# Rebuilding fp32 weights from 64-bit words: the last addition moved from GpSimd to VectorE, the sign mask made a 16-bit operation, one attention scaling moved to GpSimd

## The chip, the cores and the metric

One core of one Trainium2 chip runs the whole program. The metric is device time in microseconds (us); the median of several runs is compared. Engines are named as the profile names them: PE (TensorE matmul), PEld (its weight load), DVE (VectorE), ACT (ScalarE), POOL (GpSimd), SP (the engine that issues most DMAs). L705 is line 705 of the kernel before.

## The reference

Attention over 4 batches, 8 heads, 576 positions and 64 columns, mixed with a linear-attention memory, and then two feed-forward layers over 2304 tokens:

```python
a = softmax(causal(q @ k.T / sqrt(D)))
local = a @ v
mem_out = (phi(q) @ M_prev) / (phi(q) . z_prev)       # phi = elu + 1
x = g * mem_out + (1 - g) * local                     # 2304 x 512
h1 = x @ w_in1;  y = (s * relu(h1)**2 + b) @ w_out1   # 512 -> 2048 -> 512
h2 = y @ w_in2;  out = (h2 * tanh(softplus(h2))) @ w_out2
```

The four weight matrices of the feed-forward layers reach the core as 64-bit floats (two 32-bit words an element). Everything else is fp32.

## The kernel before, in words

The kernel splits each fp32 operand of the large products into a rounded part and a remainder ("hi" and "lo"), and TensorE makes three products in place of one.

**Stages.** The attention is cut into 32 units, one for each batch and head. Those of batch 0 are cut again into halves: eight first halves (query tiles 0 to 2, `TA`) and eight second halves (tiles 3 and 4, `TB`). These 16 are called early; their scores are plain fp32 products. The other 24 units (batches 1 to 3) run after them, in turn with the small blocks of layer 1, until about 475 us. Then come the large blocks of layer 1, and from about 620 us layer 2, whose products are written as 7 in place of 8 by combined sub-matrices.

**Conversion.** `convert` rebuilds fp32 from 64-bit words, in pieces of 128 by 512. It runs 32 times for layer 1 (to about 178 us, beside the early units) and 32 times for layer 2 (about 490 to 625 us). One piece: a DMA brings the words into a `raw` buffer; ACT scales the high word as a float (L695) into a buffer `w` of the ring `w32`, which has two slots; ACT turns the low word into a rounded integer in place (L700); DVE shifts `w` left by 3 (L702); DVE takes the sign bit of the high word and joins it to `w` (L703); POOL adds the rounded low word to `w` as an integer (L705). For layer 1, ACT then rounds `w` into the hi part (L712) and DVE subtracts for the lo part (L715); for layer 2, DVE makes sums of sub-matrices (L741), which are stored, some after a split into hi and lo (L726, L727).

**Early units.** POOL takes min(q, 0) (L498), ACT the exponential, DVE the maximum and sum (L500) and a product with a row sum for each tile (L492). PE makes the scores, DVE adds the mask and finds the least value of the row (L543), POOL writes a scaled copy of the memory's part (L555), ACT takes the exponential with a row sum (L552), DVE adjusts and inverts the sums (L572, L574). Then the rows of each tile are scaled (L569), by an engine that a letter of `E_NORM` (early units) or `F_NORM` (the others) gives for each tile: P is POOL, D is DVE, A is ACT. Tile t has 64 + 128 t columns, so 64, 192 and 320 for the tiles of a first half. PE transposes the scaled tiles (L596), ACT or DVE copies them out of PSUM (L601), and PE multiplies them with the values (L624).

**Order.** Each step has an engine, an estimated time and a priority. `Plan.order` plays the steps through with these estimates and writes down the order in which they start; each engine then runs its instructions strictly in that order. An estimate changes an order, never a duration on the chip. Conversions of layer 1 have priorities 3 to 4 apart, early units 2.36 and 8.58 apart. A first product of layer 1 can start when all eight first halves and the first weights are done; between 7 and 85 us PE is given products of zeros (L1239) where it has nothing else.

Of the kernel before, what the change touches and what calls it, by code (L numbers as in the profile page):

```python
# [11 lines left out]
BF16 = mybir.dt.bfloat16  # L12
I32 = mybir.dt.int32
U32 = mybir.dt.uint32
AF = mybir.ActivationFunctionType
ALU = mybir.AluOpType
PSUM = bass.MemoryType.PSUM
# [2 lines left out]
P = 128  # L20
MASKED = -1.0e30
HUGE = 3.0e38
SIGN = -0x80000000
PE, ACT, DVE, POOL, DMA = range(5)


# [8 lines left out]
CONV = (3.0, 3.81, 4.18, 3.12)  # L35
CONV2 = 655.2

E_TRA, E_NORM, E_XS = 'AAAADA', 'PPDDA', 'A'
F_NORM = 'PPDDA'
C_HI, C_W, C2_W = 'AAAA', 'AAAA', 'AAAA'  # L40

# [8 lines left out]
def act_us(n, extra=0):  # L50
    return 0.094 + 0.00083 * n + 0.093 * extra


def dve_us(n, fast=False):
    return 0.068 + (0.00052 if fast else 0.00104) * n


def pool_us(n):
    return 0.2 + 0.0033 * n
# [6 lines left out]
def on(letter):  # L66
    return {"A": ACT, "D": DVE, "P": POOL}[letter]
# [111 lines left out]
class Plan:  # L179
# [29 lines left out]
    def add(self, engine, us, prio, f, r=(), w=(), after=(), keep=(), share=1.0):  # L209


        bufs = list({id(b): b for b in (*r, *w, *keep) if b.ring is not None}.values())
        new = [b for b in bufs if b.maker is None]
        waits = {id(s): s for b in r for s in b.writers}
        waits.update((id(s), s) for s in after)
        s = Step(engine, us, prio, f, list(waits.values()), bufs, new)
        s.share = share
        s.left = len(waits)
        for x in waits.values():
            x.next.append(s)  # L220
        for b in bufs:
            b.users += 1
            if b.maker is None:
                b.maker = s
            elif id(b.maker) not in waits:
                b.maker.next_start.append(s)
                s.left += 1
        for b in w:
            b.writers.append(s)
        self.steps.append(s)  # L230
        return s
# [100 lines left out]
def attention_then_two_ffn(ctx: ExitStack, tc: tile.TileContext, qk, qz, vm, beta,  # L332
# [3 lines left out]
    nc = tc.nc  # L336
# [24 lines left out]
    add = plan.add  # L361
# [31 lines left out]
    nc.vector.tensor_scalar_min(igate[:, 1], igate[:, 1], 80.0)  # L393
    nc.scalar.activation(igate, igate, AF.Exp)
    nc.vector.tensor_scalar_add(igate, igate, 1.0)
# [36 lines left out]
    def unit(b, h, prio, groups=(TA, TB), place=None):  # L432
# [4 lines left out]
        def add(engine, us, f, r=(), w=(), keep=(), share=1.0):  # L437
            attention_steps.append(plan.add(engine, us, prio, f, r, w, keep=keep, share=share))
# [48 lines left out]
        def q_rows():  # L487
            return qn()[:, lo_t + 1:lo_t + n_t + 1]
# [9 lines left out]
        add(POOL, pool_us(n_t * D), lambda: nc.gpsimd.tensor_scalar_min(ex.t[:, mine], q_rows(), 0.0), [qn_b], [ex])  # L498
        add(ACT, act_us(n_t * D), lambda: nc.scalar.activation(ex.t[:, mine], ex.t[:, mine], AF.Exp), [ex], [ex])
        add(DVE, dve_us(n_t * D), lambda: nc.vector.scalar_tensor_tensor(ex.t[:, mine], q_rows(), 0.0, ex.t[:, mine],  # L500
# [26 lines left out]
        def score(t):  # L527
# [23 lines left out]
            def exp():  # L551
                nc.scalar.activation(Pt[t].t[:, D:w + D], Pt[t].t[:, D:w + D], AF.Exp, bias=mx.t[:, t + i:t + i + 1],  # L552
                                     scale=-1.0, accum_out=rs.t[:, t:t + 1])
# [5 lines left out]
        def norm(tiles):  # L559
# [4 lines left out]
            def scale(t, e):  # L564
                x, r = Pt[t].t[:, D:P * (t + 1)], rs.t[:, t:t + 1]
                if e == ACT:
                    nc.scalar.activation(x, x, AF.Copy, scale=r)
                else:
# [95 lines left out]
    def w_at(nm, r, j):  # L664
        return W[nm, r].t[:, j]
# [8 lines left out]
    def convert(layer, prio, which, r, j, raw, after=()):  # L674


        w_in, w_out = ((w_in1, w_out1), (w_in2, w_out2))[layer - 1]
        fc = r * FPR + j
        src = w_in[j * P:(j + 1) * P, r * 512:(r + 1) * 512] if which == "in" else w_out[fc * P:(fc + 1) * P, :]
        w = Buf(R["w32"], [P, 512], I32)  # L680

        def words():
            return raw.t[:, :1024].rearrange("p (n two) -> p n two", two=2)

        def f32():
            return w.t.bitcast(F32)

        add(DMA, 1.5, prio, lambda: nc.sync.dma_start(words(), src.bitcast(I32).rearrange("p (n two) -> p n two", two=2)),
            w=[raw], after=after).lag = 1.0 if layer == 1 else 3.0

        e = on((C_W if layer == 1 else C2_W)[j])
        add(e, 0.52 if e == ACT else 0.335, prio,
            (lambda: nc.scalar.activation(f32(), words()[:, :, 1].bitcast(F32), AF.Copy, scale=2.0 ** -112)) if e == ACT else  # L695
            (lambda: nc.vector.tensor_scalar(f32(), words()[:, :, 1].bitcast(F32), 2.0 ** -112, None, op0=ALU.mult)),
            [raw], [w])

        low_words = Buf()
        add(ACT, 0.52, prio, lambda: nc.scalar.activation(words()[:, :, 0], words()[:, :, 0].bitcast(U32), AF.Copy,  # L700
                                                          scale=2.0 ** -29), [raw], [low_words])
        add(DVE, 0.335, prio, lambda: nc.vector.tensor_scalar(w.t, w.t, 3, None, op0=ALU.logical_shift_left), [w], [w])  # L702
        add(DVE, 0.6, prio, lambda: nc.vector.scalar_tensor_tensor(w.t, words()[:, :, 1], SIGN, w.t,  # L703
                                                                   op0=ALU.bitwise_and, op1=ALU.bitwise_or), [raw, w], [w])
        add(POOL, 1.23 if layer == 1 else 1.45, prio, lambda: nc.gpsimd.tensor_tensor(w.t, w.t, words()[:, :, 0], op=ALU.add),  # L705
            [raw, low_words, w], [w])
        if layer == 1:
            hi, lo = f"w{which[0]}h", f"w{which[0]}l"
            hi_dve, lo_dve = C_HI[j] == "D", C_LO[j] == "D"
            half = Buf()  # L710
            add(DVE if hi_dve else ACT, 0.335 if hi_dve else 0.52, prio,
                lambda: (nc.vector.tensor_copy if hi_dve else nc.scalar.copy)(w_at(hi, r, j), f32()), [w],  # L712
                [W[hi, r], half])
            add(DVE if lo_dve else POOL, 0.6 if lo_dve else 1.23, prio,
                lambda: (nc.vector if lo_dve else nc.gpsimd).tensor_tensor(w_at(lo, r, j), f32(),  # L715
                                                                           w_at(hi, r, j).bitcast(F32), op=ALU.subtract),
                [w, half], [W[lo, r]])
        return w
# [414 lines left out]
    for i, p in enumerate(pieces):  # L1133
        convert(1, start, *p, raws[i])
        start += CONV[i // 8]
# [15 lines left out]
    for i in range(len(seq) + LAG1):  # L1151
        if i < len(seq):
# [5 lines left out]
            n = len(plan.steps)  # L1158
# [4 lines left out]
        if i >= LAG1:  # L1163
            j, fc = seq[i - LAG1]
            n = len(plan.steps)
# [3 lines left out]
            if fc == NFC - 1:  # L1169
                n = len(plan.steps)  # L1170
# [17 lines left out]
    n = len(plan.steps)  # L1188
# [3 lines left out]
    def converted_piece(which, r, j):  # L1192
        n = len(plan.steps)
        w = convert(2, CONV2, which, r, j, Buf(R["raw"], [P, 1024], I32), [opened])
        raw_steps.extend(plan.steps[n:])
        return w
# [17 lines left out]
    n = len(plan.steps)  # L1214
# [72 lines left out]
```

## Time and profile before

| | us |
|---|---|
| median of 3 runs (1041.0 to 1042.43) | 1041.44 |
| the profiled execution: its own time | 1041.25 |
| the profiled execution: span of its instructions | 1039.4 |
| busy in the span: PE | 1004.7 |
| busy in the span: DVE | 845.4 |
| busy in the span: ACT | 713.2 |
| busy in the span: POOL | 278.2 |

The span runs from the first to the last instruction of the profiled execution; 1.85 us of its own time lie around it. A busy time is the union of the engine's instructions, and an instruction that stands still because another engine keeps it from its memory still counts as busy. So a duration is read against other durations of the same instruction. PE's ends are modelled, and a busy PE is not always a PE at its peak.

### The profile page before, as it was taken

Reading aid. Unit: us, or ns where it says so; the run is one execution under the profiler, and the core shown is the slowest. Engines: PE = TensorE matmul, PEld = TensorE weight load, DVE = VectorE, ACT = ScalarE, POOL = GpSimd, SP = SyncE. Lnnn points to the kernel's source line nnn. Section 1 sums busy time; section 2 is a strip of 40 time slices with the busy share of each in tenths; the row PEclk is TensorE's granted clock in tenths of the full one; section 3 lists DMA queues with packets and bytes.
Section 4 is the critical chain, followed back from the end, with each engine's and each line's share of the span. In section 5 each row is a group of like instructions: output and inputs, shape, how many; then the busy total and the mean of one; then the engine's idle time right before and its main releaser. Section 6 shows DMA issues by size and latency. Waiting matters only on the chain.

```text
span 1039.4 us, 20180 instructions
## 1 busy us (share of the span) xinstructions
PE 1004.7 (97%) x6708; PEld 928.9 (89%) x6708; DVE 845.4 (81%) x2347; ACT 713.2 (69%) x1606; POOL 278.2 (27%) x386
## 2 busy tenths in 40 slices
PE   6889997999999999999999999999999999999998
PEld 4657787999999999999888778899999999999998
DVE  6899899999999989986568896359985789767864
ACT  6876897888988888876777897536753456434552
POOL 6864354333343334320234220000110000100010
PEclk9998998999999999999999999999999999999999
DMA  9663563323432333225888887558686766676464
GB/s 260 181 195 103 152 193 95 111 85 99 137 111 72 93 119 94 83 64 157 234 254 265 271 290 232 213 192 288 214 295 226 233 220 202 238 236 216 151 218 168
DMA packets 88984, 188.63 MB, mean 181 GB/s; under 512 B 8752, under 2 KB 63024, under 8 KB 81584
## 3 DMA queue, kind: packets, MB, share of 16 engines
q1 hardware_dynamic: 81392, 135.95, 42.3%
q0 software_dynamic: 7056, 51.38, 14.7%
q8 instruction: 53, 0.87, 0.3%
q14 instruction: 51, 0.42, 0.1%
q10 hardware_dynamic: 432, 0.01, 0.0%
HBM read 144.32 MB, written 42.99 MB: 180 GB/s over the span
## 4 chain that ended last, share of the span: by engine, by line
PE 59%; DVE 14%; issue 11%; ACT 7%; DMA 4%; POOL 3%; POOLq 0%; DVEq 0%; ACTq 0%; SPq 0%
PE bank L1003 15%; PE bank L1069 12%; PE bank L871 12%; PE bank L798 11%; PE bank L624 3%; PE bank L596 3%; DVE PTl L604 2%; PE bank L538 1%; DVE Pt L543 1%; PE bank L539 1%; DVE stage L703 1%; ACT PTh L601 1%; ACT Pt L552 1%; DVE stage L702 1%; POOL stage L705 1%
## 5 line engine op out<-in xcount | busy, mean ns | idle before, releaser
L1069 PE MATMUL bank<-woh,S 128*128 128x256 f32 x792 | 107.3, 283 | 0.0
L1069 PEld LDWEIGHTS bank<-woh,S 128*128 128x128 f32 x792 | 100.8, 192 | 0.1
L1069 PE MATMUL bank<-wol,S 128*128 128x256 f32 x720 | 98.1, 283 | 0.0
L555 POOL TENSOR_SCALAR Pt<-ex,nm 128x64 f32<-128x64 f32 x148 | 74.5, 516 | 85.1 <-PE bank L596 38.5
L1003 PE MATMUL bank<-wi,woh 128*128 128x384 f32 x426 | 94.0, 335 | 0.0
L552 ACT ACTIVATE Pt<-Pt,mx 128x64 f32<-128x64 f32 (+4 forms) x148 | 81.8, 555 | 16.5 <-DVE mx L543 15.7
L1069 PEld LDWEIGHTS bank<-wol,S 128*128 128x128 f32 x720 | 91.8, 192 | 0.0
L596 PE MATMUL bank<-ident,Pt 128*128 128x128 f32 x432 | 67.0, 281 | 10.8 <-POOL Pt L569 7.9
L1003 PEld LDWEIGHTS bank<-wi,woh 128*128 128x128 f32 x426 | 75.6, 188 | 0.6
L1003 PE MATMUL bank<-wi,wol 128*128 128x384 f32 x294 | 76.0, 335 | 0.1
L705 POOL TENSOR_TENSOR stage<-stage 128x512 int32<-128x512 int32 x36 | 48.5, 1348 | 99.6 <-DVE stage L703 50.0
L604 DVE TENSOR_TENSOR PTl<-bank,PTh 128x128 fp32r<-128x128 f32 (+1 forms) x144 | 63.8, 480 | 2.3 <-ACT PTh L601 1.2
L596 PEld LDWEIGHTS bank<-ident,Pt 128*128 128x128 f32 x432 | 49.7, 143 | 17.0 <-POOL Pt L569 10.3
L569 POOL TENSOR_SCALAR Pt<-Pt,rs 128x64 f32<-128x64 f32 x64 | 45.3, 749 | 70.7 <-DVE rs L574 54.6
L984 POOL DMA_DIRECT2D wol<-wo_split_d x17 | 9.2, 542 | 201.7 <-DVE wi L727 109.9
L543 DVE CUSTOM_DVE_ANT_0 Pt<-bank,mask 128x320 f32<-128x320 f32 (+3 forms) x148 | 59.1, 416 | 3.3 <-PE bank L539 1.6
L601 ACT CAST PTh<-bank 128x128 fp32r<-128x128 f32 (+1 forms) x144 | 54.8, 430 | 2.6 <-PE bank L596 1.7
L871 PE MATMUL bank<-gh,wol 128*128 128x256 f32 x320 | 54.0, 292 | 0.0
L871 PE MATMUL bank<-gl,woh 128*128 128x256 f32 x320 | 53.7, 290 | 0.0
L1003 PEld LDWEIGHTS bank<-wi,wol 128*128 128x128 f32 x294 | 53.0, 188 | 0.6 <-DMA wol<-wi_split_d 0.3
L871 PE MATMUL bank<-gh,woh 128*128 128x256 f32 x320 | 53.1, 289 | 0.0
L798 PE MATMUL bank<-xh,wi 128*128 128x256 f32 x320 | 50.6, 289 | 1.4 <-DVE rt L849 1.3
(278 smaller groups left out, 2961.9 us busy)
## 6 DMA issues: line engine op xcount, KB each, us to landing
wol<-wo_split_d POOLq DMA_DIRECT2D x17, 1024.0 KB, 5.2
woh<-wo_split_d POOLq DMA_DIRECT2D x16, 1024.0 KB, 5.8
qk<-in_qk SPq DMA_DIRECT2D x24, 608.0 KB, 3.9
stage<-in_w_out SPq DMA_DIRECT2D x23, 512.0 KB, 4.5
wo_split_d<-high SPq DMA_DIRECT2D x44, 256.0 KB, 3.1
stage<-in_w_in SPq DMA_DIRECT2D x21, 512.0 KB, 4.8
stage<-wi_d SPq DMA_DIRECT2D x24, 384.0 KB, 5.3
wi_split_d<-woh SPq DMA_DIRECT2D x8, 1024.0 KB, 4.9
```

The costliest lines, as they stand in the source:

```text
L543: nc.vector.tensor_tensor_reduce(Pt[t].t[:, D + lo:D + hi], ps.t[:, :hi - lo], mask[:, SP - w + lo:SP - w + hi], -SCALE, mx.t[:, t:t + 1] ...
L552: nc.scalar.activation(Pt[t].t[:, D:w + D], Pt[t].t[:, D:w + D], AF.Exp, bias=mx.t[:, t + i:t + i + 1], scale=-1.0, accum_out=rs.t[:, t:t ...
L555: add(POOL, 0.3, lambda: nc.gpsimd.tensor_scalar(Pt[t].t[:, :D], ex.t[:, t, :], nm.t[:, t:t + 1], 1.0, op0=ALU.mult, op1=ALU.mult), [ex, n ...
L569: (nc.vector if e == DVE else nc.gpsimd).tensor_scalar(x, x, r, None, op0=ALU.mult)
L596: nc.tensor.transpose(ps.t[:, c - c0, :], Pt[t].t[:, c * P:(c + 1) * P], ident)
L601: (nc.vector.tensor_copy if dve else nc.scalar.copy)(PT[0].t[:, at_], ps.t[:, :n])
L604: nc.vector.tensor_tensor(PT[1].t[:, at_], ps.t[:, :n], PT[0].t[:, at_].bitcast(F32), op=ALU.subtract)
L705: add(POOL, 1.23 if layer == 1 else 1.45, prio, lambda: nc.gpsimd.tensor_tensor(w.t, w.t, words()[:, :, 0], op=ALU.add), [raw, low_words, ...
L798: nc.tensor.matmul(ph, w_at(nm, r, cc)[:, o:o + P], x_at(x, cc), start=(part == 0 and cc == 0), stop=(part == 2 and cc == NCC - 1))
L871: nc.tensor.matmul(acc[ec // per].t[:, (ec % per) * n:(ec % per + 1) * n], w_at(nm, r, jj)[:, ec * P:(ec + 1) * P], t(x), start=(big and f ...
L1003: nc.tensor.matmul(ps.t[:, :H2], w[i // 4].t[:, j, kk, i % 4], x[kk].t[:, k], start=begin and part == kk == 0, stop=part == 2 and kk == 1, ...
L1069: nc.tensor.matmul(acc[t].t[:, :DH], s.t[:, j, t * P:(t + 1) * P], x.t[:, k, q % 4], start=q == part == 0, stop=q == NQ2 - 1 and part == 2)
```

## The change

The integer addition of a conversion goes from GpSimd to VectorE. The sign bit no longer goes into `w` by a 32-bit operation with two inputs: a 16-bit operation takes the top 16 bits of the high word, keeps bit 15, and writes it into the top 16 bits of the rounded low word, so that the addition brings the sign along. This operation waits for ACT's rounding of the low word (L700), whose result it writes into; the addition waits for it. The scaling of tile 2 of the eight first halves (320 columns) goes from VectorE to GpSimd (`E_NORM`). The estimates that the planner uses change with the steps, and with them the orders of all engines.

```diff
+U16 = mybir.dt.uint16
-SIGN = -0x80000000
-E_TRA, E_NORM, E_XS = 'AAAADA', 'PPDDA', 'A'
+E_TRA, E_NORM, E_XS = 'AAAADA', 'PPPDA', 'A'
...
+        def limbs():
+            return raw.t[:, :1024].bitcast(U16).rearrange("p (n four) -> p n four", four=4)
+
...
         add(DVE, 0.335, prio, lambda: nc.vector.tensor_scalar(w.t, w.t, 3, None, op0=ALU.logical_shift_left), [w], [w])
-        add(DVE, 0.6, prio, lambda: nc.vector.scalar_tensor_tensor(w.t, words()[:, :, 1], SIGN, w.t,
-                                                                   op0=ALU.bitwise_and, op1=ALU.bitwise_or), [raw, w], [w])
-        add(POOL, 1.23 if layer == 1 else 1.45, prio, lambda: nc.gpsimd.tensor_tensor(w.t, w.t, words()[:, :, 0], op=ALU.add),
-            [raw, low_words, w], [w])
+        signed = Buf()
+        add(DVE, 0.335, prio, lambda: nc.vector.tensor_scalar(limbs()[:, :, 1], limbs()[:, :, 3], 0x8000, None, op0=ALU.bitwise_and),
+            [raw, low_words], [signed])
+        add(DVE, 0.75, prio, lambda: nc.vector.tensor_tensor(w.t, w.t, words()[:, :, 0], op=ALU.add), [raw, signed, w], [w])
```

## Rows read from the trace of the kernel before

**Rows 1.** Busy time of each engine by stretch (busy us, count; TensorE clock, DMA)
```profile
0.00:60.00 60.00, 48.39 (x236) 33.39 (x237) 47.24 (x189) 43.99 (x125) 49.05 (x71) 1.00 0.76 216
60.00:180.00 120.00, 106.88 (x675) 88.06 (x674) 112.70 (x326) 95.52 (x220) 52.40 (x61) 0.95 0.48 146
...
250.00:300.00 50.00, 49.66 (x399) 48.17 (x398) 48.05 (x185) 42.69 (x115) 19.38 (x31) 1.00 0.38 111
```

**Rows 2.** The chain that ended last, 0:60 and 60:180, shares by line
```profile
by line: POOL stage L705 7.2%; POOL Pt L569 7.1%; DMA wil<-in_w_out 6.9%; POOL Pt L555 5.5%; issue 4.1%; POOL ex L498 3.7%; DVE stage L703 2.8%; DVE wol L492 2.5%; PE bank L534 2.5%; PE bank L596 2.3%; POOL B L555 1.8%; PE bank L1239 0.6%; 
...
by line: issue 10.6%; PE bank L798 7.2%; PE bank L871 6.1%; DVE stage L703 6.1%; PE bank L624 5.6%; DVE Pt L543 4.4%; PE bank L534 4.1%; DVE stage L702 3.7%; DVE qn L492 3.6%; DMA wil<-in_w_out 3.5%; DVE wil L715 2.9%; DVE gl L854 2.2%; DVE
```

**Rows 3.** Busy time by stretch of the additions of L705 alone
```profile
0.00:60.00 60.00, 13.28 (x10) 1.00 0.76 216
60.00:180.00 120.00, 28.93 (x22) 0.95 0.48 146
```

**Rows 4.** Timeline of VectorE and of GpSimd near 92 us (start, us, instruction)
```profile
92.21 1.76 DVE L715 TENSOR_TENSOR wil<-stage,wih 128x512 fp32r<-128x512 f32 x1
...
92.13 1.29 POOL L705 TENSOR_TENSOR stage<-stage 128x512 int32<-128x512 int32 x1 [1.61 <-ACT wih L712]
```

**Rows 5.** Instructions by line and form, VectorE, 0:180 (busy us, mean ns, idle before)
```profile
L702 DVE TENSOR_SCALAR stage<-stage 128x512 int32<-128x512 int32 x32 | 17.0, 535 | 1.6 <-ACT stage L695 1.3
L703 DVE SCALAR_TENSOR_TENSOR stage<-stage 128x512 int32<-128x512 int32 x22 | 16.2, 737 | 0.2
L715 DVE TENSOR_TENSOR wol<-stage,woh 128x512 fp32r<-128x512 f32 x16 | 12.8, 797 | 0.2 <-ACT woh L712 0.2
L492 DVE CUSTOM_DVE_ANT_0 qn<-ex,qn 128x64 f32<-128x64 f32 x31 | 8.3, 315 | 0.1
...
L715 DVE TENSOR_TENSOR wil<-stage,wih 128x512 fp32r<-128x512 f32 x8 | 7.1, 885 | 0.9 <-ACT wih L712 0.7
...
L715 DVE TENSOR_TENSOR wi<-stage,wi 128x512 fp32r<-128x512 f32 x8 | 6.4, 794 | 0.0
...
L572 DVE TENSOR_SCALAR rs<-rs,igate 128x2 f32<-128x2 f32 x10 | 5.7, 572 | 1.0 <-ACT Pt L552 0.8
...
L569 DVE TENSOR_SCALAR Pt<-Pt,rs 128x448 f32<-128x448 f32 x6 | 4.6, 763 | 0.1
```

**Rows 6.** The same view, VectorE, 180:480
```profile
L492 DVE CUSTOM_DVE_ANT_0 qn<-ex,qn 128x64 f32<-128x64 f32 x105 | 17.1, 219 | 0.4
...
L569 DVE TENSOR_SCALAR Pt<-Pt,rs 128x448 f32<-128x448 f32 x22 | 9.9, 451 | 0.0
...
L572 DVE TENSOR_SCALAR rs<-rs,igate 128x2 f32<-128x2 f32 x22 | 4.9, 223 | 0.6 <-ACT Pt L552 0.5
```

**Rows 7.** One line's instructions, L702 and L817 (ns min/median/max, first and last start)
```profile
L702 DVE TENSOR_SCALAR stage<-stage x52: 389/422/1537, 8.6 to 622.0; 128x512 int32<-128x512 int32 x52
...
L817 DVE TENSOR_TENSOR yl<-yr,yh x8: 677/683/693, 481.8 to 583.0; 128x512 fp32r<-128x512 f32 x8
```

**Rows 8.** Timeline of VectorE near 64 us
```profile
63.62 0.40 DVE L702 TENSOR_SCALAR stage<-stage 128x512 int32<-128x512 int32 x1
63.94 0.44 DVE L569 TENSOR_SCALAR Pt<-Pt,rs 128x448 f32<-128x448 f32 x1
```

**Rows 9.** Instructions by line and form, GpSimd, 180:480
```profile
L498 POOL TENSOR_SCALAR ex<-qn 128x320 f32<-128x320 f32 x21 | 23.1, 1102 | 42.0 <-DMA qn<-in_qz 38.2 <-DVE Pt L569 3.9
L569 POOL TENSOR_SCALAR Pt<-Pt,rs 128x192 f32<-128x192 f32 x22 | 18.5, 839 | 0.0
```

**Rows 10.** The same view, GpSimd, 0:180
```profile
L569 POOL TENSOR_SCALAR Pt<-Pt,rs 128x192 f32<-128x192 f32 x10 | 11.0, 1097 | 0.0
```

**Rows 11.** The same view, VectorE, 0:60
```profile
L569 DVE TENSOR_SCALAR B<-B,rs 128x320 f32<-128x320 f32 x4 | 1.6, 394 | 0.0
```

**Rows 12.** Who waited for whom, GpSimd, 0:180 (us, times, longest)
```profile
POOL stage L705 <- ACT stage L700: 5.3, 2, 4.0
```

**Rows 13.** Who waited for whom, TensorE, 470:700
```profile
PE bank L798 <- ACT yh L816: 1.7, 3, 0.6
```

## The prediction

> **What bounds the kernel now.** I read the busy times by stretch first. From 250 to 300 us, as in the whole stretch in which attention alternates with layer 1, PE is busy for 49.66 of 50 us [rows 1]; the change touches nothing there, so a microsecond won or lost earlier should pass straight to the end. Before 180 us it is otherwise. From 60 to 180 us PE is busy for 106.88 of 120 us and its weight loads for only 88.06, while DVE is busy for 112.70. From 0 to 60 us no engine is full: POOL has 49.05, DVE 47.24, ACT 43.99 [rows 1].
>
> The chain of waits says which of them counts. In the first 60 us its costliest entries are POOL's: the additions of L705, the scalings of L569, the copies of L555 and the minima of L498. From 60 to 180 us POOL's lines are gone from the head of the list, and DVE's conversion and attention lines stand among PE's [rows 2]. So I treat the first 60 us as set by POOL, with DVE close behind, and the next 120 us as set by DVE.
>
> Then I compared durations of equal instructions. At 92.21 us a subtraction of L715 takes 1.76 us on DVE; the same kind of instruction (128 by 512, two SBUF inputs) takes 0.683 elsewhere [rows 4, 7]. POOL's addition ran from 92.13 to 93.42, and the subtraction ended 0.55 us after it: it stood still until the addition was over. The Trainium skill, SBUF — State Buffer, section "SBUF: two separate sides", has the same picture: VectorE and GpSimd arbitrate for one port pair, an exclusive lock held for a whole instruction. The trace agrees with 1.76 against 0.683 us.
>
> **What these stalls cost before 180 us.** Eight forms carry enough of it to be read, against their undisturbed durations: the shift L702, 32 by (0.535 - 0.422) = 3.6 us; L715, 16 by (0.797 - 0.683) = 1.8, 8 by (0.885 - 0.683) = 1.6, 8 by (0.794 - 0.683) = 0.9; L703, 22 by (0.737 - 0.683) = 1.2; L572, 10 by (0.572 - 0.223) = 3.5; L569 at 448 columns, 6 by (0.763 - 0.451) = 1.9; L492, 31 by (0.315 - 0.219) = 3.0 [rows 5 to 7]. Together 17.5 us. The undisturbed values of three of them are from 180 to 480 us, where POOL still runs one-input work (19.38 us of 50) but no addition [rows 1, 6]. So I charge the 17.5 us to the 32 additions, 42.2 us of POOL time, and split it by their busy time: 5.5 us before 60 us and 12.0 us after [rows 3]. Bounds: half of it, if one-input work on POOL is to blame for the rest, and 25 us, an estimate, six tenths of the additions' time.
>
> **The change, part by part.** On DVE each instruction starts about 0.08 us before the one ahead has ended (0.40 us long, the next 0.32 us later) [rows 8], so on DVE's path an instruction counts its duration less 0.08.
>
> *The sign operation* is new on DVE, 32 times a layer. The trace has no 16-bit operation at a stride. The nearest row below is the shift, one input and 512 columns, 0.422 us (0.389 at the fastest); the nearest above is a two-input operation of 512 columns, 0.683 [rows 7]. I take 0.42, since like the shift it has one SBUF input and one SBUF output: 0.34 us on the path; the other end is 0.60. The Trainium skill, VectorE: DVE Perf Modes, section "What auto-detection actually checks", grants two columns a cycle to one source in SBUF by its outer count and names no condition on the stride, which would be the 0.42; no run here has shown it for such a stride, and at one column a cycle the sum would be that of the second rival.
>
> *The addition replaces L703*: two inputs and 512 columns both, so I count nothing. The diff's own estimates are 0.75 against 0.60; the upper bound is those 0.15 us.
>
> *The scaling of tile 2* leaves DVE eight times at 0.394 us, 0.31 on the path: -2.5 us [rows 11]. On POOL 320 columns with one input take 1.10 us after 180 us; the 192-column scaling takes 0.839 there and 1.097 before 180 us, 1.31 times as much [rows 9, 10]. So I take 1.44 us, eight times 11.5 us, with 1.10 (8.8 us) as the other end.
>
> *The additions leave POOL*: 13.3 us before 60 us, 28.9 after [rows 3]. Behind a waiting addition POOL's attention work had to stand; that goes too.
>
> *The new wait*: the sign operation needs L700 on ACT. POOL waited for that in 2 places, 5.3 us in all [rows 12]; now it would be DVE, with everything queued there behind it. The planner puts other DVE work in between, and ACT has 24.5 us free after 60 us [rows 1], so I count nothing; without that cover it is up to these 5.3 us.
>
> **The sum.** Before 60 us, 10 conversions: DVE +3.4 - 2.5 - 5.5 = -4.6 us, POOL -13.3 + 11.5 = -1.8. POOL sets this part, so I take -1.8. From 60 to 180 us, 22 conversions: DVE +7.5 - 12.0 = -4.5 us, and DVE sets it. Together -6.3 us. In layer 2 the additions also leave POOL, but PE waited there for 1.7 us in its largest group only, for ACT's copies [rows 13]; DVE's gain has nothing to shorten, and I count 0, with 1.7 us as the other end. 1041.25 - 6.3 = 1034.95 for the profiled execution; the median lies 0.19 above that execution's own time, so 1035.1 us.
>
> **Rivals.**
> *The eight scalings hold up the first halves (slower).* Each first half would wait 1.44 - 0.31 = 1.13 us longer for its third tile, 9.0 us in all, and layer 1 cannot start before the last of them. For it: L569 on POOL is as large on the chain of the first 60 us as L705 [rows 2]. Against it: the additions leave the same queue. It decides if these additions had only filled POOL's gaps; then +9.0 - 4.5 = +4.5, 1045.9 us. It is slower from the point where the first part loses over 4.5 us.
>
> *The sign operation runs at one column a cycle.* Then it costs 0.60 on the path: from 60 to 180 us +13.2 - 12.0 = +1.2, before 60 us +6.0 - 2.5 - 5.5 = -2.0 (POOL -1.8): together -0.6, 1040.8 us, no change. With the addition at the 0.15 us more as well, +4.5 from 60 to 180 us and -0.5 before, 1045.4 us.
>
> *One-input work on POOL stalls DVE as the additions did.* The 17.5 us of stall for 42.2 us of additions are 0.41 us for each; 11.5 us of scalings would cost DVE 4.8 us, DVE in the first 60 us would be at +0.2 in place of -4.6, and nothing is won there: -4.5, 1036.9 us. The lock of the Trainium skill's page SBUF — State Buffer, same section, holds for any GpSimd instruction and would have it so; the undisturbed durations beside 19.38 us of such work in 50 speak against it [rows 1, 6].
>
> *More than the sum.* If POOL's queue does not set the first part, all of -4.6 counts there, and 1.7 us in layer 2: -10.8, 1030.6 us.
>
> **How the numbers follow.** The forecast 0.58, the scalings 0.12, the sign operation at one column a cycle 0.12 and with the slow addition 0.05, one-input stalls 0.08, more than the sum 0.05. A measurement of this kernel can tell about 0.2% from no change, 2.1 us. Faster: 0.58 + 0.08 + 0.05 = 0.71; same 0.12; slower 0.12 + 0.05 = 0.17. The range for 8 in 10 goes below to the sum with 25 us of stalls (7.5 more, which with the first part still set by POOL is 5.1: 1030.0), and two microseconds for the new orders, 1028; above to 1043, which takes in the case without change and leaves out the two slow ones. The forecast's own range is 1030 to 1039.
>
> **What the profile after would show.** The shift, L715, L572 and L492 before 180 us at 0.42, 0.68, 0.22 and 0.22 us: the stalls are gone; if not, the main term is wrong. The sign operation at 0.42 or at 0.68 us: the second rival. The new addition at 0.68 us. Eight POOL scalings of 320 columns at 1.1 to 1.5 us, and the first subtraction L817 of layer 1 no later than now: if it is later, the first rival. DVE busy between 60 and 180 us about as full as now, but over a stretch that ends 4 to 7 us sooner. The forecast fails above all if DVE's saved time is given back in waits for ACT, or if the first part is lost in POOL's queue.

## The result and the profile after

The changed kernel takes 1025.07 us in the median of 4 runs (1022.67 to 1026.47), the kernel before 1041.22 us in the median of 4 (1039.37 to 1042.43). The ratio is 0.9837, its 95% interval 0.9816 to 0.9857. So it is faster by 16 us, where 6.3 were forecast, and lies outside the predicted range. The profiled execution took 1026.47 us with a span of 1024.7, 14.7 less than before.

All lines behind the conversion have moved by 3: the shift L702 is L705, the subtraction L715 is L718, the products L798 and L871 are L801 and L874. L707 is the sign operation, L709 the addition.

Busy time of each engine by stretch, after (columns as in [rows 1]):

```profile
0.00:60.00 60.00, 48.26 (x233) 34.41 (x233) 45.47 (x186) 43.81 (x123) 42.01 (x63) 0.91 0.78 223
60.00:180.00 120.00, 115.91 (x771) 96.13 (x772) 114.11 (x384) 102.71 (x241) 35.70 (x52) 1.00 0.50 151
```

From 60 to 180 us PE is busy for 115.9 us in place of 106.9 [rows 1] and starts 771 products in place of 675, while DVE is as full as it was (114.1 against 112.7) and starts 384 instructions in place of 326. DVE did more instructions in the same busy time. The mean granted clock of TensorE rose from 0.95 to 1.00 in this stretch (1.00 is 2.4 GHz) and fell from 1.00 to 0.91 in the one before it.

The chain of waits from 60 to 180 us, after:

```profile
by line: PE bank L624 16.2%; PE bank L801 14.8%; PE bank L874 14.7%; PE bank L534 12.6%; PE bank L596 8.3%; issue 3.5%; PE bank L1242 2.7%; DVE Pt L543 2.2%; DVE stage L709 2.1%; DVE stage L707 1.7%; PE bank L538 1.5%; PE bank L539 1.5%; AC
```

The conversion and attention lines of DVE that stood among PE's in [rows 2] are down to about 2% each; PE's own products now lead.

Instructions by line and form on VectorE, 0 to 180 us, after (columns as in [rows 5]):

```profile
L707 DVE TENSOR_SCALAR stage<-stage 128x512 uint16<-128x512 uint16 x22 | 16.3, 768 | 0.7 <-ACT stage L703 0.7
L709 DVE CUSTOM_DVE_ANT_0 stage<-stage 128x1024 uint16<-128x1024 uint16 x22 | 15.0, 684 | 0.1
L705 DVE TENSOR_SCALAR stage<-stage 128x512 int32<-128x512 int32 x32 | 13.7, 437 | 1.3 <-ACT stage L698 1.3
L718 DVE TENSOR_TENSOR wol<-stage,woh 128x512 fp32r<-128x512 f32 x16 | 11.0, 688 | 0.3 <-ACT woh L715 0.2
...
L492 DVE CUSTOM_DVE_ANT_0 qn<-ex,qn 128x64 f32<-128x64 f32 x36 | 6.3, 227 | 0.0
...
L569 DVE TENSOR_SCALAR Pt<-Pt,rs 128x448 f32<-128x448 f32 x6 | 2.7, 448 | 0.0
...
L572 DVE TENSOR_SCALAR rs<-rs,igate 128x2 f32<-128x2 f32 x10 | 2.3, 231 | 0.3 <-ACT Pt L552 0.3
```

Beside [rows 5]: the shift is at 437 ns in place of 535, the subtraction at 688 in place of 797, the product with a row sum at 227 in place of 315, the 448-column scaling at 448 in place of 763, the two-column L572 at 231 in place of 572. In these forms the stalls are gone. The sign operation takes 0.756 us in the median (row below), longer than either value in the prediction; the addition takes 0.684 us, as predicted.

One line's instructions after (ns min/median/max, first and last start): the sign operation, and the first subtraction of layer 1, L820. The row below is that subtraction before, L817.

```profile
L707 DVE TENSOR_SCALAR stage<-stage x44: 731/756/845, 9.5 to 606.5; 128x512 uint16<-128x512 uint16 x44
...
L820 DVE TENSOR_TENSOR xl<-xr,xh x20: 410/416/458, 78.6 to 412.6; 128x256 fp32r<-128x256 f32 x20
```

```profile
L817 DVE TENSOR_TENSOR xl<-xr,xh x20: 409/416/507, 74.1 to 428.3; 128x256 fp32r<-128x256 f32 x20
```

Instructions by line and form on GpSimd, 0 to 180 us, after: the eight new scalings take 1.40 and 1.21 us.

```profile
L569 POOL TENSOR_SCALAR Pt<-Pt,rs 128x320 f32<-128x320 f32 x4 | 5.6, 1398 | 0.0
...
L569 POOL TENSOR_SCALAR B<-B,rs 128x320 f32<-128x320 f32 x4 | 4.8, 1212 | 0.0
```

To see where along the span the time was won I use one line of products: the weight loads for the remainders of the large blocks of layer 1. I call the starts of the first and of the last of them the two marks. The first starts when attention and the small blocks are over, the last at the end of layer 1; the conversions of layer 2 run between them. First before, then after:

```profile
L871 PEld LDWEIGHTS bank<-xl,woh x96: 186/188/333, 509.7 to 690.7; 128*128 128x128 f32 x96
```

```profile
L874 PEld LDWEIGHTS bank<-xl,woh x96: 187/188/189, 497.9 to 675.4; 128*128 128x128 f32 x96
```

So 11.8 us are won up to the first mark (509.7 to 497.9), 3.5 between the marks (181.0 to 177.5 us), and 0.6 lost behind them: 14.7. Each of these is read from one execution. Behind the last mark four kernels with one and the same order (before and the second attempt, below) differ by up to 3.1 us, so 0.6 us can't be told from nothing and 3.5 barely.

### The profile page after: what moved, and what is told of

It is laid out like the page before. It is cut to its first block, busy times and chain, and to the rows that moved or that the text cites. A ratio compares the mean times of both kernels' runs of the same rounds, so it can differ in the third digit from the quotient of the medians.

```text
span 1024.7 us, 20147 instructions
## 1 busy us (share of the span) xinstructions
PE 1000.5 (98%) x6738; PEld 927.6 (91%) x6738; DVE 840.1 (82%) x2403; ACT 713.2 (70%) x1606; POOL 203.9 (20%) x330
## 4 chain that ended last, share of the span: by engine, by line
PE 70%; DVE 9%; issue 7%; DMA 6%; ACT 5%; POOL 2%; SPq 0%; POOLq 0%; DVEq 0%; ACTq 0%
PE bank L1006 15%; PE bank L1072 14%; PE bank L874 13%; PE bank L801 13%; PE bank L624 5%; PE bank L596 4%; PE bank L534 2%; DMA wi_d<-sc 2%; PE bank L538 1%; PE bank L539 1%; POOL Pt L569 1%; DMA stage<-in_w_in 1%; DMA woh<-wo_split_d 1%; PE bank L1242 1%; DMA x_d<-xs 1%
## 5 line engine op out<-in xcount | busy, mean ns | idle before, releaser
L569 POOL TENSOR_SCALAR Pt<-Pt,rs 128x64 f32<-128x64 f32 (+2 forms) x68 | 52.4, 806 | 77.1 <-DVE rs L574 44.6
L874 PE MATMUL bank<-gl,woh 128*128 128x256 f32 x320 | 53.2, 289 | 0.0
L874 PE MATMUL bank<-gh,wol 128*128 128x256 f32 x320 | 53.2, 288 | 0.0
L874 PE MATMUL bank<-gh,woh 128*128 128x256 f32 x320 | 52.3, 286 | 0.0
L801 PE MATMUL bank<-xh,wi 128*128 128x256 f32 x320 | 50.1, 287 | 0.3 <-DVE rt L852 0.2
L624 PE MATMUL bank<-PTh,V 128*128 128x384 f32 (+1 forms) x192 | 48.1, 277 | 0.0
```

The source lines that it names most:

```text
L569: (nc.vector if e == DVE else nc.gpsimd).tensor_scalar(x, x, r, None, op0=ALU.mult)
L624: nc.tensor.matmul(o.rearrange("p (t q) -> p t q", q=P), v, x.t[:, f[0]:f[-1] + 1:f[1] - f[0] if len(f) > 1 else 1, :], start=(c == 0 and ...
L801: nc.tensor.matmul(ph, w_at(nm, r, cc)[:, o:o + P], x_at(x, cc), start=(part == 0 and cc == 0), stop=(part == 2 and cc == NCC - 1))
L874: nc.tensor.matmul(acc[ec // per].t[:, (ec % per) * n:(ec % per + 1) * n], w_at(nm, r, jj)[:, ec * P:(ec + 1) * P], t(x), start=(big and f ...
```

## The experiments

Each median stands against the kernel before on the same chip.

**Which part of the change counts.** Four kernels: the change without the scaling (`E_NORM` left at `PPDDA`), the scaling alone, and the new conversion in one layer only.

```diff
 # conversion_only, against after (scaling_only, against before, is the reverse)
-E_TRA, E_NORM, E_XS = 'AAAADA', 'PPPDA', 'A'
+E_TRA, E_NORM, E_XS = 'AAAADA', 'PPDDA', 'A'
 # layer1_only, against after, in convert (layer2_only: layer == 2, and 'PPDDA')
+        if layer == 1:
             signed = Buf()
...
+        else:
+            add(DVE, 0.6, prio, lambda: nc.vector.scalar_tensor_tensor(w.t, words()[:, :, 1], SIGN, w.t,
+                                                                       op0=ALU.bitwise_and, op1=ALU.bitwise_or), [raw, w], [w])
+            add(POOL, 1.23 if layer == 1 else 1.45, prio, lambda: nc.gpsimd.tensor_tensor(w.t, w.t, words()[:, :, 0], op=ALU.add),
+                [raw, low_words, w], [w])
```

> The change without its scaling (tile 2 of the first halves stays on VectorE). If the additions that leave GpSimd carry the gain (the theory), about 1025 to 1030 us. If the scaling on GpSimd carries a good part (rival), 1033 us or more.

> The kernel before with the scaling of tile 2 of the first halves on GpSimd, the additions still there. Theory: GpSimd's queue is the fuller by 11 us while VectorE is relieved of 2.5 us, so 1041 to 1047 us. Rival (VectorE's relief counts first): 1036 to 1040 us.

> The new conversion and the scaling in layer 1, the old conversion in layer 2 (32 pieces each). In the trace of the changed kernel layer 1's products run some 12 us earlier by 540 us and 15 us at the end. Theory: 1028 to 1031 us. Rival (half of the gain is made in layer 2's conversions): 1033 us or more.

> The old conversion and scaling in layer 1, the new conversion in layer 2 alone. Theory: 2 to 4 us, 1037 to 1039 us. My prediction's step (nothing to shorten there): 1041 us.

| | us | before | ratio, 95% interval |
|---|---|---|---|
| conversion_only | 1025.40 | 1042.11 | 0.9843, 0.9815 to 0.9870 |
| scaling_only | 1039.84 | 1042.11 | 0.9985, 0.9969 to 1.0001 |
| layer1_only | 1026.11 | 1042.11 | 0.9854, 0.9833 to 0.9874 |
| layer2_only | 1037.26 | 1042.11 | 0.9954, 0.9936 to 0.9972 |

The scaling neither wins nor loses anything that can be told, alone or beside the new conversion. In conversion_only the first subtraction of layer 1 starts at 65.5 us (row below), with the scalings on GpSimd at 78.6: layer 1 begins 13 us later with them, and the end is the same.

```profile
L820 DVE TENSOR_TENSOR xl<-xr,xh x20: 404/418/457, 65.5 to 411.4; 128x256 fp32r<-128x256 f32 x20
```

The new conversion in layer 1 alone (with the scaling) brings 16.0 us, more than was expected of it, and that in layer 2 alone 4.8. The two don't add up (20.8 against 16 together). On top of layer 1's, layer 2's adds 1.0 us by the medians (1026.11 against 1025.07), and the intervals of the two ratios overlap: beside the new conversion in layer 1, no gain is shown for layer 2.

The rows of layer 2: busy time from 575 to 625 us, columns as in [rows 1], of before, of layer2_only, of after and of layer1_only.

```profile
575.00:625.00 50.00, 47.81 (x199) 38.13 (x198) 45.12 (x84) 44.78 (x92) 16.20 (x11) 0.97 0.88 281
```

```profile
575.00:625.00 50.00, 49.83 (x220) 40.72 (x219) 41.49 (x93) 43.66 (x91) 0.00 (x0) 1.00 0.86 281
```

```profile
575.00:625.00 50.00, 50.00 (x223) 41.39 (x222) 41.55 (x92) 43.24 (x91) 0.00 (x0) 1.00 0.84 283
```

```profile
575.00:625.00 50.00, 48.80 (x215) 40.04 (x214) 46.09 (x89) 44.52 (x94) 12.91 (x9) 1.00 0.88 286
```

Before, PE starts 199 products there; without GpSimd's additions 220 and 223. It had lost 2.2 us as idle time, and more by the clock, 0.97 in the mean. The prediction had looked at the largest group of waits alone [rows 13]. But layer1_only still has the additions on GpSimd in layer 2, and it starts 215 products at a clock of 1.00. The marks of layer1_only, and of scaling_only, which has the additions too:

```profile
L881 PEld LDWEIGHTS bank<-xl,woh x96: 187/188/189, 497.0 to 673.2; 128*128 128x128 f32 x96
```

```profile
L871 PEld LDWEIGHTS bank<-xl,woh x96: 187/188/188, 507.0 to 684.9; 128*128 128x128 f32 x96
```

Between their marks it is 176.2 and 177.9 us, as short as the 177.5 of after. Their orders are other than that of before, so the 3.5 us that after wins there can't be put down to the additions that left GpSimd in layer 2.

**First attempt: the suspected cost put back into the new kernel.** Three kernels add a GpSimd instruction to each conversion, after the sign operation: of one column (the wait alone), of 384 columns with one input, and a two-input integer addition. A fourth issues the new addition on GpSimd, every engine otherwise in the order of after. The added instructions were not in the plan that sets the orders.

```diff
 # against after, behind L709: one_input_beside (wait_one_column has 1 in place of 384)
+        add(NONE, 0.0, prio, lambda: nc.gpsimd.tensor_scalar(words()[:, :384, 1].bitcast(F32), words()[:, :384, 1].bitcast(F32), 1.0, None, op0=ALU.mult), [raw, signed])
 # addition_beside
+        add(NONE, 0.0, prio, lambda: nc.gpsimd.tensor_tensor(words()[:, :, 1], words()[:, :, 1], words()[:, :, 0], op=ALU.add), [raw, signed])
 # addition_on_gpsimd: nc.vector.tensor_tensor in L709 becomes nc.gpsimd.tensor_tensor
```

> The changed kernel with one more GpSimd instruction for each conversion: a multiplication of one column by 1, which waits for the sign operation as the addition did, and which nothing but the raw buffer's release waits for. The other engines keep the changed kernel's order. Theory (what cost time was VectorE standing still while an addition held the memory port): 1025 to 1027 us. Rival (GpSimd's own queue: attention work stood behind an addition that waited): 1031 us or more, with GpSimd idle for the sign operation.

> The same place and wait, but the instruction multiplies 384 columns by 1: one input, about as long on GpSimd as the addition was. Theory: VectorE's stalls before 180 us stay under 8 us, 1026 to 1030 us. Rival (any GpSimd work stalls VectorE as the additions did): stalls of 15 us or more, 1032 us or more.

> The same place and wait, but a whole integer addition of two inputs and 512 columns, whose result nobody reads. VectorE keeps its own addition. Theory: the stalls are back, 18 to 25 us before 180 us and as much between 480 and 630 us, on top of the sign operation, 1037 to 1050 us. Rival (the stalls were off the path): under 1031 us.

> The changed kernel, planned as it is, so with the same order on all engines but the two, but the addition itself is issued on GpSimd. VectorE is relieved of 0.6 us for each of 64 conversions, some 19.5 us before 180 us, and gets the stalls back, some 20 us. By VectorE's sum alone: no change, 1024 to 1028 us. If the two further changes of engine and GpSimd's queue in the chain of a conversion count too: 1032 us or more. If the order is what won (rival): 1028 us or less as well, so that a higher time speaks against the order.

| | us | before | ratio, 95% interval |
|---|---|---|---|
| wait_one_column | 1032.03 | 1042.61 | 0.9893, 0.9861 to 0.9926 |
| one_input_beside | 1053.66 | 1042.61 | 1.0102, 1.0083 to 1.0122 |
| addition_beside | 1061.64 | 1042.61 | 1.0177, 1.0162 to 1.0193 |
| addition_on_gpsimd | 1050.49 | 1042.61 | 1.0074, 1.0058 to 1.0091 |

By the ratios the one column, little more than a wait, costs 6 us. The first three were misses for the theory, whose times were 1025 to 1027, 1026 to 1030 and 1037 to 1050 us: even a one-input instruction cost some 28 us. Who waited for whom, TensorE, 0 to 180 us, one_input_beside and then after:

```profile
PE bank L596 <- POOL Pt L569: 14.8, 11, 3.5
```

```profile
PE bank L596 <- POOL Pt L569: 5.7, 8, 1.9
```

PE's transposes wait for the scalings on GpSimd, which stand behind the added instruction and behind what that waits for. The times of these kernels measure a full in-order queue, not the stalls.

Their traces show the stalls all the same. In wait_one_column, one_input_beside and addition_beside VectorE runs the same instructions as in after, in the same order, so its busy time can be read up to one and the same instruction, the end of the last subtraction of layer 1's conversion (stretch, its length, busy, count; clock, DMA):

```profile
0.00:173.53 173.53, 150.18 (x523) 0.97 0.59 175
```

```profile
0.00:193.17 193.17, 155.52 (x523) 0.91 0.53 157
```

```profile
0.00:195.92 195.92, 168.26 (x523) 0.91 0.53 155
```

Beyond the one column, the one-input instruction stalls VectorE by 5.3 us and the addition by 18.1. Both read their inputs at a step of two words here, so that step is not what sets the addition apart. The stretch itself is only 2.8 us longer with the addition than with the one-input instruction (195.92 and 193.17), and both are some 20 us longer than with the one column.

The time of addition_on_gpsimd says something on the question of the order: with the orders of after, and 0.68 us less of VectorE work in each conversion, it is 25 us slower than the change. So the new orders by themselves don't make the gain.

**Second attempt: in place, in the order of before.** Now GpSimd's instruction keeps its place, its waits and its planned time, and only its kind changes. one_input_in_place puts a one-input multiplication over 400 columns there, one_column_in_place over one column. addition_on_vector_before_order keeps the place in the plan, but VectorE executes the addition.

```diff
 # line 705 of before; the planned engine and time stay as they are
-  lambda: nc.gpsimd.tensor_tensor(w.t, w.t, words()[:, :, 0], op=ALU.add),
+  lambda: nc.gpsimd.tensor_scalar(f32()[:, :400], f32()[:, :400], 1.0, None, op0=ALU.mult),  # one_input_in_place
+  lambda: nc.gpsimd.tensor_scalar(f32()[:, :1], f32()[:, :1], 1.0, None, op0=ALU.mult),      # one_column_in_place
+  lambda: nc.vector.tensor_tensor(w.t, w.t, words()[:, :, 0], op=ALU.add),                   # addition_on_vector_before_order
```

> The kernel before, in exactly its own order, but the instruction that GpSimd runs in place of the integer addition has one input: it multiplies 400 columns by 1, about as long as the addition. The low words are left out. Wait, place in GpSimd's queue and time on GpSimd stay; only the stalls of VectorE should go, from about 17 us to under 8 before 180 us and from 20 to under 10 between 480 and 630 us. Theory (the stalls carry the gain): 1034 us or less. Rival (GpSimd's queue and the longer chain of a conversion carry it): 1038 us or more.

> The same with one column in place of 400: the wait and the place in the queue stay, GpSimd's time and VectorE's stalls go. The low words are left out. Theory of the stalls: within 3 us of the run with 400 columns. Rival: 6 us or more below it, some 1026 to 1030 us.

> The kernel before, in its own order, old sign operation, but the integer addition issued on VectorE: 0.6 us more on VectorE for each conversion, 19.5 us before 180 us, the stalls gone, and no GpSimd instruction in the chain. By VectorE's sum, as I worked it out in the prediction, no change: 1040 to 1044 us. If the chain and GpSimd's queue count beside the sum: 1030 to 1036 us. If it reaches 1026 us, neither the new sign operation nor the new order has won anything.

| | us | before | ratio, 95% interval |
|---|---|---|---|
| one_input_in_place | 1020.09 | 1042.19 | 0.9790, 0.9763 to 0.9817 |
| one_column_in_place | 1018.32 | 1042.19 | 0.9772, 0.9749 to 0.9795 |
| addition_on_vector_before_order | 1026.46 | 1042.19 | 0.9850, 0.9823 to 0.9878 |

The first answers the question of the cause. Its instruction by line and form on GpSimd, 0 to 180 us:

```profile
L705 POOL TENSOR_SCALAR stage<-stage 128x400 f32<-128x400 f32 x32 | 40.8, 1274 | 45.0 <-DVE stage L703 33.0 <-DVE nm L504 6.8 <-DVE rs L572 3.7
```

That is 40.8 us of GpSimd, where the 32 additions took 42.2 [rows 3], in the same place and with the same waits, and 22 us are gone. Not only VectorE is relieved by it: GpSimd's other instructions up to the second cut below take 53.2 us in all in place of 58.4. VectorE runs the same instructions in the same order in the first two kernels and in the one before (in the third 64 additions more), so its busy time can be read up to one and the same instruction. The first cut lies in a shift L702 near 60 us, just before the next instruction starts, the second at the end of the last L715, which ends the conversion of layer 1; an instruction that lies across a cut counts on both sides. Busy time of VectorE between them (stretch, its length, busy, count; clock, DMA), of before, one_input_in_place, one_column_in_place and addition_on_vector_before_order:

```profile
0.00:59.90 59.90, 47.15 (x188) 1.00 0.76 216
59.90:178.06 118.16, 110.92 (x323) 0.95 0.48 148
```

```profile
0.00:57.53 57.53, 41.38 (x188) 1.00 0.78 221
57.53:162.86 105.33, 98.52 (x323) 0.98 0.55 168
```

```profile
0.00:55.60 55.60, 39.95 (x188) 1.00 0.79 228
55.60:160.03 104.43, 95.19 (x323) 0.98 0.56 170
```

```profile
0.00:168.66 168.66, 152.99 (x542) 0.99 0.62 180
```

The same instructions keep VectorE busy for 158.07, 139.90 and 135.15 us in the first three. The additions' stalls are therefore 18.2 us beyond those of a one-input instruction of nearly the same length, and 22.9 beyond those of one column (8.3 us of GpSimd in all). Counted from one column, the one-input instruction stalls VectorE too, but by 4.8 us where the addition stalls it by 22.9. And up to the cut 15.2 and 18.0 us are won.

The fourth shows the other side. The 32 additions on VectorE raise its busy time from 135.15 to 152.99, by 17.8 us, and the cut comes 8.6 us later (160.03 to 168.66): about half. The other half came out of VectorE's idle time, 24.9 us up to the cut in one_column_in_place and 15.7 with the additions. Over the whole span the two kinds of busy time can be set side by side: with the additions on VectorE it is busy for 843.7 us (row below), before for 845.4. It is as busy, in the same order, and 15.7 us faster, where VectorE's sum as the prediction worked it out gave no change. With the old sign operation and the old order it comes as far (0.9850) as the change (0.9837): the new sign operation and the new orders win nothing that can be told.

Busy time, share of the span and count, addition_on_vector_before_order:

```profile
PE 999.5 (97%) x6708; PEld 926.7 (90%) x6708; DVE 843.7 (82%) x2411; ACT 712.8 (69%) x1606; POOL 192.0 (19%) x322
```

The marks in layer 1, for one_input_in_place, one_column_in_place and addition_on_vector_before_order:

```profile
L871 PEld LDWEIGHTS bank<-xl,woh x96: 187/188/189, 492.8 to 668.8; 128*128 128x128 f32 x96
```

```profile
L871 PEld LDWEIGHTS bank<-xl,woh x96: 187/188/188, 489.5 to 665.2; 128*128 128x128 f32 x96
```

```profile
L871 PEld LDWEIGHTS bank<-xl,woh x96: 186/188/188, 500.5 to 676.5; 128*128 128x128 f32 x96
```

Between the marks it is 176.0, 175.7 and 176.0 us, against 181.0 before: by these traces the stalls of layer 2 cost 5 us in the order of before, and the additions on VectorE nothing that can be told.

**Is added work cheap because it lies off the chain?** vector_work_beside is one_column_in_place with a two-input instruction of 512 columns more on VectorE in each conversion, on which only the release of the raw buffer waits. old_sign is the changed kernel with the old sign operation (L703 of before) ahead of the new addition.

```diff
 # vector_work_beside, against one_column_in_place, behind L703 (which also writes the Buf joined)
+        add(NONE, 0.0, prio, lambda: nc.vector.scalar_tensor_tensor(words()[:, :, 1], words()[:, :, 1], SIGN, words()[:, :, 0], op0=ALU.bitwise_and, op1=ALU.bitwise_or), [raw, joined, low_words])
 # old_sign, against after
-        signed = Buf()
-        add(DVE, 0.335, prio, lambda: nc.vector.tensor_scalar(limbs()[:, :, 1], limbs()[:, :, 3], 0x8000, None, op0=ALU.bitwise_and),
-            [raw, low_words], [signed])
+        add(DVE, 0.6, prio, lambda: nc.vector.scalar_tensor_tensor(w.t, words()[:, :, 1], SIGN, w.t, op0=ALU.bitwise_and, op1=ALU.bitwise_or), [raw, w], [w])
```

> The kernel before in its own order, one column in place of the addition on GpSimd (the low words are left out), and for each conversion one more two-input operation of 0.69 us on VectorE, whose result nobody reads and for which no conversion waits. It stands beside the run with one column (1018.3 us) and the run with the addition itself on VectorE (1026.5 us). If VectorE has slack for work that stands in its order (theory: 39 us of it cost 8), 1024 to 1028 us. If added work costs its full time and the addition on VectorE was only paid for by a shorter chain (rival), 1033 us or more.

> The changed kernel with the sign joined as before, by a 32-bit operation of 0.69 us that does not wait for ScalarE's rounding, in place of the 16-bit one of 0.76 us that does. Planned with its own estimates. If the sign operation's length and wait cost something, 1020 to 1023 us; if not, 1024 to 1027 us.

vector_work_beside took 1026.42 us (before 1043.49; 0.9836, 0.9821 to 0.9850), the same as the additions in the chain, 0.9850. So it is the room in VectorE's order that takes the work up, not a chain grown shorter or longer. old_sign took 1027.87 us (before 1043.49; 0.985, 0.983 to 0.987), a little above both times that were expected, and not to be told from the change (0.9837): the sign operation, 0.756 us in place of 0.69 and with a wait for ACT, costs nothing measurable.

**A version with less work on VectorE.** The sign is joined to the low word (L707 below), and one instruction shifts `w` and joins both, in place of three.

```diff
 # joined_by_or, in place of L705, L707 and L709 of after; ACT's low word with bias=-0.5
+        add(DVE, 0.6, prio, lambda: nc.vector.scalar_tensor_tensor(words()[:, :, 0], words()[:, :, 1], SIGN, words()[:, :, 0], op0=ALU.bitwise_and, op1=ALU.bitwise_or), [raw, low_words], [signed])
+        add(DVE, 0.6, prio, lambda: nc.vector.scalar_tensor_tensor(w.t, w.t, 3, words()[:, :, 0], op0=ALU.logical_shift_left, op1=ALU.bitwise_or), [raw, signed, w], [w])
 # joined_by_or_old_scaling: the same with E_NORM 'PPDDA'
```

> A version that may beat both: the sign goes into the low word by a 32-bit operation with two inputs, and shift and joining are one two-input operation, an or, so that VectorE runs two instructions of 0.69 us in place of three; ScalarE rounds the low word down (bias -0.5), since an or carries nothing. Last bits are cut off in place of rounded. VectorE is relieved of some 0.41 us for each conversion, 13 us in each layer: 1012 to 1022 us if VectorE still counts, 1023 to 1027 if TensorE sets everything after 60 us by now.

> The version joined by or, with tile 2 of the first halves scaled by VectorE as before. GpSimd's queue of the first 60 us is shorter by 11 us, VectorE's longer by 2.5. If GpSimd's queue sets the first 60 us now: 1016 to 1021 us; if not, 1022 to 1025 us.

They took 1022.95 us (before 1042.19; 0.9812, 0.9785 to 0.9839) and 1025.52 us (before 1043.49; 0.9810, 0.9778 to 0.9842). Both intervals overlap the change's, so a gain over the changed kernel isn't shown, and the first time lies between the two that were to tell whether VectorE still counts.

## Why the prediction was right in sign and wrong in size

**Right: the cause and its undisturbed durations.** The change wins because GpSimd's two-input addition is gone, which makes VectorE stand still; one_input_in_place shows it with that instruction alone changed. Most of what it frees is VectorE's time (18.2 us up to the cut, against 5.2 of GpSimd's other work). The addition on VectorE (0.68 us forecast, 0.684 measured) and the scalings on GpSimd (1.1 to 1.5 forecast, 1.40 and 1.21 measured) came out as priced. The lower bound, that one-input work on POOL is to blame for half of the stalls, fell: with such work in the additions' place 4.8 of 22.9 us stay.

**The step that failed most: the stalls before 180 us, sized too small.** The prediction took -1.8 for the first 60 us (POOL's sum, with the scalings in it) and -12.0 for the next 120. one_column_in_place, whose instructions are those of before, shows VectorE relieved of 7.2 us (47.15 to 39.95) and then of 15.7 (110.92 to 95.19), where eight forms had given 5.5 and 12.0. The time fell by 4.3 us in the first part (59.90 to 55.60), by 13.7 in the second (118.16 to 104.43), and by another 2.2 up to the first mark of layer 1 (18.0 at the cut, 20.2 at the mark). That is -20.2 in place of -13.8. "POOL sets this part" does not hold as a sum: in one_column_in_place POOL is 13.1 us less busy in the first part (48.95 to 35.85), VectorE 7.2, and the part is 4.3 us shorter. What does set it the runs don't show: in one_input_in_place POOL is 3.0 us less busy there, VectorE 5.8, and the part is 2.4 us shorter.

**The added work: a wrong duration and a wrong price that cancel, by luck.** The sign operation was taken at 0.42 us and measures 0.756, more than the other end of 0.683. At the full price that the prediction charged, 22 of them would have cost 22 x (0.756 - 0.08) = 14.9 us and not 7.5. But VectorE took about half of such work into its idle time (8.6 of 17.8 us). From one_column_in_place to after the first mark moves from 489.5 to 497.9, by +8.4 us for addition, sign operation, scaling and order together, close to the +7.5 that the prediction counted for the second part. The step "DVE sets it" held for stalls in the second part, 13.7 us for 15.7, and not for work.

**Layer 2: counted 0.** "DVE's gain has nothing to shorten" read the largest group of waits alone, where a window of 50 us shows PE 2.2 us short and at a clock of 0.97, and it is wrong for layer 2 by itself: layer2_only wins 4.8 us. Between the marks the change wins 3.5 us, 2.9 with what is lost behind them. Whether that comes from layer 2's additions is not shown, since layer1_only, which keeps them, has it too.

**The balance.** 6.4 us more from the stalls, 0.9 less for the work, 2.9 from the first mark on: 8.4 us, and the profiled execution came out at 1026.47 where 1034.95 were forecast.

**The rivals.** The scalings hold up the first halves: what the prediction named as its sign happened, layer 1 begins at 78.6 us and not at 74.1, but it costs nothing (conversion_only has the old scaling and the same time). The sign operation at one column a cycle: its duration is even longer than that rival took it, and its price did not come (old_sign). One-input work stalls VectorE as the additions did: false, by 4.8 us against 22.9. The Trainium skill, SBUF — State Buffer, section "SBUF: two separate sides", states the lock on the port pair for a GpSimd instruction of any kind. The trace agrees with that for the additions, and for the one-input instruction only to 4.8 us; the measurement decides. More than the sum: this is what came, in kind: a first part that POOL's sum does not give, and a gain from the first mark on. Its chance of 0.05 was too small, and its 1030.6 us still too long.

**What stays open.** Why a microsecond of stall costs 0.79 us up to the cut (18.0 / 22.9), and one of added work 0.48 (8.6 / 17.8). Before, the stalls strike short attention instructions that others wait for (L572 at 572 ns for 231) while added work stands where its order has room; that this is the reason is argued, not shown. Nor was the share of TensorE's clock separated: it was 0.95 from 60 to 180 us before and 1.00 after, but PE's work differs there too, and no run held one of them fixed. What made the stretch of layer 2 shorter in the change, the additions that are gone or the new order, is open too. And the addition differs from the one-input instructions in more than its inputs: it has 512 columns for 400 or 384, and 32-bit integers for fp32. No run separated these.

## What to carry to other kernels

Busy time that is stall and busy time that is work are not worth the same: with nearly equal VectorE totals (845.4 and 843.7 us) two kernels lay 15.7 us apart, so add up a stall as the excess over the same instruction undisturbed, in all forms and in every stage, and look for it beside two-input additions on GpSimd. To test a suspected cost, change the instruction in place and keep order, queue and waits; with an instruction put beside the others the time measures the queue. Where two prices are unknown, look also at the idle time of the engine: work that is added in its order is paid first from there.

## What was not expected of the hardware

Counted from 32 instructions of one column, 32 one-input GpSimd instructions of 1.27 us hold VectorE up by 4.8 us, 32 two-input integer additions of 1.32 us by 22.9; in the order of after it is 5.3 and 18.1. The 16-bit operation with one input, 512 columns at a step of four 16-bit elements, takes 0.756 us on VectorE, nearly twice the 0.42 of the dense 32-bit shift [rows 7]; whether the step or the 16 bits cost it, no run separated. For one source in SBUF the Trainium skill, VectorE: DVE Perf Modes, section "What auto-detection actually checks", names two columns a cycle by the outer count and no condition on the step, which would have put it near the shift. The trace disagrees, with 0.756 us.
